# Moving the two-column carry copies of a fused attention and convolution kernel from GpSimd to ScalarE

## The chip, the cores and the metric

The kernel runs on one core of one Trainium2 chip. The metric is the device time of one execution in microseconds; the time before is the median of three runs.

## The reference

Eight batches (B = 8) of 8 heads with 512 tokens (x) and 32 state tokens (state), 64 wide, go through three blocks:

```python
# 1: attention between tokens and state, both ways
xread = softmax(scale * x @ state.T) @ state        # 512 rows per batch
sread = softmax(scale * state @ x.T) @ x            # 32 rows per batch
x = concatenate([xread, sread], axis=2)             # 544 rows per batch, 512 wide
# 2: gated convolution over the rows
h = maximum(x @ w_in, 0)                            # 1024 wide
conv_out = sum over k of conv_w[k] * hp[:, k:k + S] # 3 taps, hp is h with a zero row at each end
x = (h * sigmoid(conv_out)) @ w_out
# 3: a mix with the row before, then two products and a gate
k = maximum(xk @ w_k, 0); v = (k * k) @ w_v
out = sigmoid(xr @ w_r) * v
```

All arithmetic is held near float32: matrix products are made from a high and a low part of each operand, three products for one.

## The kernel before, in words

The second block is the part that the diff touches. Its rows are cut into nine tiles: tile t = 0 to 7 holds the 512 token rows of batch t, and the last tile (t = 8) holds the 32 state rows of all eight batches side by side. The 1024 columns of h are cut into eight groups f of 128, one group on the 128 partitions, so there are 72 slots (t, f), each of which passes these stages:

- `g1_main`: TensorE makes the product into the PSUM tile `hps`.
- `g1_a` (lines 486 to 512): GpSimd writes zeros to the first and last column of `hb` (L491), ScalarE writes relu of `hps` between them (L492), and GpSimd copies the last two columns of the block into `carry` (L493). In the last tile the two columns that precede each batch's 32 state rows are copied from `carry` into `hb` (L496, eight blocks of two columns), the pads behind them are zeroed (L497) and ScalarE writes the relu (L498). Then ScalarE makes the first tap of the convolution (L508, tile `cacc`) and VectorE adds the other two (L510).
- `g1_b`: ScalarE makes the tanh (L519), VectorE the gate (L520).
- `g1_c`: ScalarE makes the high part `gs` (L528); the low part (L530) is made by GpSimd for tiles 0 to 2 and by VectorE for the rest.
- `g1_sec`: TensorE multiplies `gs` by the output weights into the four accumulators `acc`; after the last f they are evicted (L549, L551) and stored.

`hb` has three buffers, so a slot's `hb` is free once VectorE's gate (L520) of three slots before has read it. The carry of all eight batches is read only in the last tile.

Between the slots the attention of the following batches is worked off in pieces (half slots): scores, maxima, exponentials (L361, L367, L377, L388 among them), and `pair_m`, which evicts a product (L283 on ScalarE, L284 on VectorE) and sends it to its place by four DMAs on SyncE's queue (L287). The next batch's `hps` reads it (tiles `me`, `m_odd`).

The order of instructions on each engine is not the order of the source. Each stage gets a priority, and a planner orders the queues along a timeline that it simulates itself:

```python
tc.cur_priority = BASE + 1000 * (i - d) + STAGE[k]                    # L1248
with _tile.TileContext(nc, schedule_with_timeline_sim=True) as tc:    # L1311
```

The third block (first 16 slots of the same form, then a stage of seven products per tile) doesn't contain the changed lines.

Of the kernel before, what the change touches and what calls it, by code (L numbers as in the profile page):

```python
# [11 lines left out]
AF = mybir.ActivationFunctionType  # L12
# [23 lines left out]
def tile_kernel(  # L36
# [26 lines left out]
    nc = tc.nc  # L63
    B, P, NST, H, D = x_n.shape
    KC, S = x_t.shape[1], x_t.shape[3]
# [54 lines left out]
    carry = const.tile([P, KF, B, 2], F32, name="carry")  # L120
# [339 lines left out]
    def width(t):  # L460
        return S if t < B else B * Z - 2
# [24 lines left out]
    def g1_a(t, f):  # L486
        n = width(t)
        s = st1[t, f]
        hb = s["hb"] = cp.tile([P, N + 2], F32, tag="hb", name="hb", bufs=3)
        if t < B:  # L490
            nc.gpsimd.memset(hb[:, 0:S + 2:S + 1], 0.0)  # L491
            nc.scalar.activation(hb[:, 1:1 + S], s["p"], AF.Relu)  # L492
            nc.gpsimd.tensor_copy(carry[:, f, t], hb[:, S - 1:S + 1])  # L493
        else:
            v = hb[:, :B * Z].rearrange("p (b n) -> p b n", b=B)
            nc.gpsimd.tensor_copy(v[:, :, 0:2], carry[:, f])  # L496
            nc.gpsimd.memset(v[:, :, NS + 2:], 0.0)  # L497
            nc.scalar.activation(  # L498
                v[:, :, 2:NS + 2], s["p"][:, :B * NS].rearrange("p (b n) -> p b n", b=B), AF.Relu
            )  # L500
        if t == 0 and f < CONV_ON_PE:
            a = s["a"] = ps_h.tile([P, 512], F32, tag="h", name="cps")
            for k in range(3):
                nc.tensor.matmul(a, diag[:, 3 * f + k], hb[:, k:k + S], start=k == 0, stop=k == 2)
            return
        a = s["a"] = cp.tile([P, N], F32, tag="acc", name="cacc")
        w = [vcol[:, k * KF + f:k * KF + f + 1] for k in range(3)]
        nc.scalar.activation(a[:, :n], hb[:, 0:n], AF.Copy, scale=w[0])  # L508
        for k in (1, 2):
            nc.vector.scalar_tensor_tensor(  # L510
                a[:, :n], hb[:, k:k + n], w[k], a[:, :n], op0=ALU.mult, op1=ALU.add
            )
# [682 lines left out]
    ]  # L1195
    end = len(slots)
    FN = {1: (g1_main, g1_a, g1_b, g1_c, g1_sec), 2: (g2_main, g2_a, g2_b, g2_c, g2_sec)}
    p2 = None
    for i in range(len(slots) + 2):
        if i < len(slots):  # L1200
            ph, t, f = slots[i]
# [113 lines left out]
```

## Time and profile before

| | |
|---|---|
| median of 3 runs | 848.87 us (847.53 to 849.36) |
| profiled execution | 847.36 us, of which 845.6 us lie between its first and last instruction |
| busy in the span: TensorE, VectorE, ScalarE, GpSimd | 815.8, 719.9, 601.3, 108.7 us |
| mean granted clock of TensorE | 0.993 |

The busy time of an engine is the union of its instructions; an engine that is busy all the time may still be slowed by waits inside, since ends of matmuls are modelled. The chain of waits is the chain of work that ended last, followed back from the last instruction of the program: at each step to what released it, or to the instruction before it on its engine. PE is TensorE's matmul, PEld its weight load, DVE is VectorE, ACT is ScalarE, POOL is GpSimd, SP is SyncE.

### The profile page before, as it was taken

Reading aid. Unit: us, or ns where it says so; the run is one execution under the profiler, and the core shown is the slowest. Engines: PE = TensorE matmul, PEld = TensorE weight load, DVE = VectorE, ACT = ScalarE, POOL = GpSimd, SP = SyncE. Lnnn points to the kernel's source line nnn. Section 1 sums busy time; section 2 is a strip of 40 time slices with the busy share of each in tenths; the row PEclk is TensorE's granted clock in tenths of the full one; section 3 lists DMA queues with packets and bytes.
Section 4 is the critical chain, followed back from the end, with each engine's and each line's share of the span. In section 5 each row is a group of like instructions: output and inputs, shape, how many; then the busy total and the mean of one; then the engine's idle time right before and its main releaser. Section 6 shows DMA issues by size and latency. Waiting matters only on the chain.

```text
span 845.6 us, 15284 instructions
## 1 busy us (share of the span) xinstructions
PE 815.8 (96%) x5670; PEld 718.1 (85%) x5670; DVE 719.9 (85%) x1143; ACT 601.3 (71%) x1035; POOL 108.7 (13%) x220
## 2 busy tenths in 40 slices
PE   5899999899989999999999989999999999999997
PEld 2466787678767877889989889999999999999997
DVE  6999987798999997989999889896978869696673
ACT  6787575586577756878877779767776876776652
POOL 2235453341111211211000000000000000000000
PEclk8999999999999999999999999999999999999999
DMA  9441436427673556405634765777778677775675
GB/s 335 143 152 51 153 92 192 126 68 207 216 214 125 177 173 205 194 3 200 228 121 162 251 235 172 253 240 246 252 227 268 214 237 262 221 257 180 220 240 205
DMA packets 82698, 163.10 MB, mean 193 GB/s; under 512 B 17600, under 2 KB 53440, under 8 KB 79808
## 3 DMA queue, kind: packets, MB, share of 16 engines
q1 hardware_dynamic: 82624, 162.12, 58.8%
q8 instruction: 45, 0.74, 0.4%
q14 instruction: 29, 0.24, 0.1%
HBM read 118.55 MB, written 30.97 MB: 177 GB/s over the span
## 4 chain that ended last, share of the span: by engine, by line
PE 74%; DVE 12%; DMA 6%; ACT 4%; issue 2%; SPq 2%; DVEq 0%; ACTq 0%; POOL 0%; POOLq 0%
PE acc L132 11%; PE acc L133 11%; PE acc L134 11%; PE vps L133 6%; PE vps L132 6%; PE vps L134 6%; PE rps L132 3%; PE rps L133 3%; PE rps L134 3%; PE hps L132 3%; PE hps L134 2%; PE hps L133 2%; DVE cacc L510 2%; DMA yt<-y 2%; DMA me<-m 1%
## 5 line engine op out<-in xcount | busy, mean ns | idle before, releaser
L510 DVE SCALAR_TENSOR_TENSOR cacc<-hb,vcol,cacc 128x512 f32<-128x512 f32 (+1 forms) x138 | 105.1, 775 | 6.2 <-ACT cacc L508 5.5
L133 PE MATMUL acc<-gs,out 128*128 128x512 f32 (+1 forms) x288 | 110.1, 384 | 0.2 <-POOL gs L530 0.2
L134 PE MATMUL acc<-gs,out 128*128 128x512 f32 (+1 forms) x288 | 109.0, 381 | 0.0
L132 PE MATMUL acc<-gs,out 128*128 128x512 f32 (+1 forms) x288 | 95.9, 385 | 0.8 <-ACT gs L528 0.8
L132 PEld LDWEIGHTS acc<-gs,out 128*128 128x128 f32 x288 | 53.0, 188 | 14.5 <-ACT gs L528 2.3
L132 PE MATMUL acc<-xo,k 128*128 128x256 f32 x224 | 63.2, 283 | 1.8 <-ACT xc L880 1.3
L133 PEld LDWEIGHTS acc<-gs,out 128*128 128x128 f32 x288 | 54.2, 188 | 10.9 <-POOL gs L530 0.6
L134 PEld LDWEIGHTS acc<-gs,out 128*128 128x128 f32 x288 | 54.2, 188 | 10.4 <-issue 0.5
L134 PE MATMUL acc<-xo,k 128*128 128x256 f32 x224 | 63.0, 282 | 0.0
L133 PE MATMUL acc<-xo,k 128*128 128x256 f32 x224 | 62.9, 281 | 0.0
L519 ACT ACTIVATE g<-cacc 128x512 f32<-128x512 f32 (+1 forms) x69 | 41.8, 606 | 24.8 <-DVE cacc L510 19.2
L528 ACT ACTIVATE gs<-g 128x512 fp32r<-128x512 f32 (+1 forms) x72 | 43.6, 607 | 21.9 <-DVE g L520 14.1
L520 DVE SCALAR_TENSOR_TENSOR g<-g,hb 128x512 f32<-128x512 f32 (+1 forms) x72 | 49.4, 686 | 1.8 <-ACT g L519 1.3
L492 ACT ACTIVATE hb<-hps 128x512 f32<-128x512 f32 x64 | 37.7, 593 | 17.8 <-PE hps L134 14.5
L508 ACT ACTIVATE cacc<-hb,vcol 128x512 f32<-128x512 f32 (+1 forms) x69 | 48.1, 703 | 1.3
L132 PE MATMUL acc<-xo,kT 128*128 128x256 f32 x168 | 47.8, 284 | 1.0 <-ACT acc L876 1.0
L133 PE MATMUL vps<-va,xa 128*128 128x256 f32 x168 | 47.6, 283 | 0.0
L132 PE MATMUL vps<-va,xa 128*128 128x256 f32 x168 | 47.5, 283 | 0.0
L134 PE MATMUL vps<-va,xa 128*128 128x256 f32 x168 | 47.5, 283 | 0.0
L133 PE MATMUL acc<-xo,kT 128*128 128x256 f32 x168 | 47.5, 283 | 0.0
L134 PE MATMUL acc<-xo,kT 128*128 128x256 f32 x168 | 47.5, 283 | 0.0
L493 POOL COPY carry<-hb 128x2 f32<-128x2 f32 x64 | 32.2, 504 | 97.2 <-ACT hb L492 97.0
(290 smaller groups left out, 2807.3 us busy)
## 6 DMA issues: line engine op xcount, KB each, us to landing
va<-vdT SPq DMA_DIRECT2D x38, 512.0 KB, 4.5
va<-vdB SPq DMA_DIRECT2D x28, 512.0 KB, 4.3
vb<-vdT SPq DMA_DIRECT2D x18, 512.0 KB, 4.6
xT<-x_t SPq DMA_DIRECT2D x32, 256.0 KB, 5.0
xn<-x_n SPq DMA_DIRECT2D x8, 1024.0 KB, 5.2
y<-yo SPq DMA_DIRECT2D x8, 1024.0 KB, 5.0
vb<-vdB SPq DMA_DIRECT2D x14, 512.0 KB, 4.2
va<-rdT SPq DMA_DIRECT2D x14, 512.0 KB, 4.5
```

The costliest lines, as they stand in the source:

```text
L132: nc.tensor.matmul(ps, lh, rh, start=start and k == 0, stop=False, **how)
L133: nc.tensor.matmul(ps, lh, rl, start=False, stop=False, **how)
L134: nc.tensor.matmul(ps, ll, rh, start=False, stop=stop and k == last, **how)
L492: nc.scalar.activation(hb[:, 1:1 + S], s["p"], AF.Relu)
L493: nc.gpsimd.tensor_copy(carry[:, f, t], hb[:, S - 1:S + 1])
L508: nc.scalar.activation(a[:, :n], hb[:, 0:n], AF.Copy, scale=w[0])
L510: nc.vector.scalar_tensor_tensor(a[:, :n], hb[:, k:k + n], w[k], a[:, :n], op0=ALU.mult, op1=ALU.add)
L519: nc.scalar.activation(g[:, :n], s["a"][:, :n], AF.Tanh, scale=0.5)
L520: nc.vector.scalar_tensor_tensor(g[:, :n], g[:, :n], 1.0, s["hb"][:, 1:1 + n], op0=ALU.add, op1=ALU.mult)
L528: act = nc.scalar.activation(gs[:, 0, :n], s["g"][:, :n], AF.Copy)
```

## The change

Both copies, the one into `carry` in tiles 0 to 7 (64 of them, 128x2) and the one out of it in the last tile (8 of them, 128x16), are made by an ACTIVATE of ScalarE with the function Copy in place of GpSimd's tensor_copy. The place in the source and the priority stay.

```diff
@@ g1_a @@
         if t < B:
             nc.gpsimd.memset(hb[:, 0:S + 2:S + 1], 0.0)
             nc.scalar.activation(hb[:, 1:1 + S], s["p"], AF.Relu)
-            nc.gpsimd.tensor_copy(carry[:, f, t], hb[:, S - 1:S + 1])
+            nc.scalar.activation(carry[:, f, t], hb[:, S - 1:S + 1], AF.Copy)
         else:
             v = hb[:, :B * Z].rearrange("p (b n) -> p b n", b=B)
-            nc.gpsimd.tensor_copy(v[:, :, 0:2], carry[:, f])
+            nc.scalar.activation(v[:, :, 0:2], carry[:, f], AF.Copy)
             nc.gpsimd.memset(v[:, :, NS + 2:], 0.0)
```

## Rows read from the trace of the kernel before

**Rows 1.** The page: busy time of the engines, and the chain by engine.

```profile
PE 815.8 (96%) x5670; PEld 718.1 (85%) x5670; DVE 719.9 (85%) x1143; ACT 601.3 (71%) x1035; POOL 108.7 (13%) x220
...
PE 74%; DVE 12%; DMA 6%; ACT 4%; issue 2%; SPq 2%; DVEq 0%; ACTq 0%; POOL 0%; POOLq 0%
```

**Rows 2.** Busy time by stage: stretch, length, then PE, PEld, DVE, ACT, POOL.

```profile
20.00:72.00 52.00, 47.27 (x244) 27.36 (x242) 51.82 (x67) 39.92 (x59) 17.41 (x18) 0.96 0.43 149
72.00:135.00 63.00, 62.81 (x439) 50.89 (x440) 56.55 (x89) 42.98 (x78) 29.20 (x49) 1.00 0.34 104
135.00:250.00 115.00, 110.08 (x721) 85.10 (x719) 100.41 (x177) 74.51 (x130) 29.43 (x56) 1.00 0.56 165
250.00:400.00 150.00, 147.91 (x882) 122.55 (x875) 139.91 (x240) 111.71 (x197) 27.16 (x71) 1.00 0.47 160
```

**Rows 3.** The same stretches for L493 alone: POOL busy and its copies.

```profile
20.00:72.00 52.00, 5.73 (x6) 0.96 0.43 149
...
135.00:250.00 115.00, 8.35 (x19) 1.00 0.56 165
```

**Rows 4.** The chain of waits, 135 to 250 us and later: start, length, what.

```profile
by line: DVE cacc L510 11.8%; issue 8.2%; SPq L287 7.5%; DMA m_odd<-m 7.3%; DVE g L520 7.2%; DMA me<-m 6.7%; DMA xT<-x_t 4.4%; DVE gs L530 3.4%; DVE s L385 3.3%; DVE m L284 2.6%; DVE q L357 2.3%; DVE s L360 2.1%; DVE s L348 2.1%; ACT m L283
...
157.61 4.39 DMA me<-m
...
184.44 0.49 ACT hb L492
...
197.94 6.06 DMA m_odd<-m
...
207.16 0.50 ACT hb L492
...
242.73 3.32 DMA me<-m
...
330.77 0.60 ACT hb L492
```

**Rows 5.** GpSimd's groups: busy, mean ns, then its idle time and what ended it.

```profile
L493 POOL COPY carry<-hb 128x2 f32<-128x2 f32 x64 | 32.2, 504 | 97.2 <-ACT hb L492 97.0
...
L496 POOL COPY hb<-carry 128x16 f32<-128x16 f32 x8 | 6.0, 745 | 20.2 <-DVE g L520 20.2
```

**Rows 6.** The tile carry: durations of its copies, and the only engine that waited.

```profile
L493 POOL COPY carry<-hb x64: 178/358/2459, 23.1 to 362.8; 128x2 f32<-128x2 f32 x64
...
  ACT g L519: 0.2, 1
```

**Rows 7.** ScalarE in order of time: start, duration, what.

```profile
3.03 0.22 ACT L178 ACTIVATE mid<-raw 128x24 f32<-128x24 f32 x1 [1.02 <-DMA raw<-conv]
3.16 0.21 ACT L180 ACTIVATE raw<-raw 128x24 uint32<-128x24 uint32 x1
...
265.65 0.19 ACT L367 ACTIVATION_READ_ACCUMULATOR e<-p_s,s 128x1 f32 x1
265.75 0.68 ACT L367 ACTIVATE e<-p_s,s 128x512 f32<-128x512 f32 x1
...
333.59 0.58 ACT L492 ACTIVATE hb<-hps 128x512 f32<-128x512 f32 x1
334.20 0.73 ACT L508 ACTIVATE cacc<-hb,vcol 128x512 f32<-128x512 f32 x1
```

**Rows 8.** A carry copy on GpSimd, and VectorE in order of time.

```profile
335.99 0.91 POOL L493 COPY carry<-hb 128x2 f32<-128x2 f32 x1 [0.98 <-ACT hb L492]
...
336.77 0.75 DVE L510 SCALAR_TENSOR_TENSOR cacc<-hb,vcol,cacc 128x512 f32<-128x512 f32 x1
337.43 0.69 DVE L520 SCALAR_TENSOR_TENSOR g<-g,hb 128x512 f32<-128x512 f32 x1
...
343.62 0.75 DVE L510 SCALAR_TENSOR_TENSOR cacc<-hb,vcol,cacc 128x512 f32<-128x512 f32 x1
344.29 0.69 DVE L520 SCALAR_TENSOR_TENSOR g<-g,hb 128x512 f32<-128x512 f32 x1
```

## The prediction

> **What bounds the kernel now.** I read the page first: TensorE is busy 96% of the span and takes 74% of the chain of waits, VectorE 12%, DMA 6%, ScalarE 4%, and GpSimd rounds to nothing [rows 1]. An average over stages with different limits is no price, so I then cut the stretch in which the changed lines run, 20 to 400 us, by stage [rows 2]. The reader is to see two kinds of stage there. From 72 to 135 us and from 250 to 400 us TensorE has work nearly without a break (62.8 of 63 us, 147.9 of 150 us): what another engine does there costs nothing until a weight load has to wait. From 20 to 72 us VectorE is the one without a break (51.8 of 52 us). From 135 to 250 us none is full (PE 110, VectorE 100, ScalarE 75 of 115 us), and the chain [rows 4] shows why: it hops from VectorE to SyncE's queue, to the landing of the small product that `pair_m` sends (4.39, 6.06 and 3.32 us), and back. Only in these two stages, 167 us together, can the change touch the path directly.
>
> Then I read who makes the copies and who needs them. The 64 copies into `carry` occupy GpSimd for 32.2 us, but before them it sat idle for 97.0 us, waiting for ScalarE's relu [rows 5]. Nobody waits for them but one tanh, once, for 0.2 us [rows 6]; the real reader is the last tile.
>
> **The change, part by part.**
>
> *GpSimd loses 64 + 8 copies*, 32.2 + 6.0 us of busy time [rows 5]. It is idle 87% of the span and the chain spends about 0% on it, so its own time is worth nothing. What stood behind a copy in its queue (the zeros of the next `hb`, the low parts of tiles 0 to 2) starts earlier by at most the copy, whose median is 0.36 us; the waits that this could shorten are not on the chain. I take 0.
>
> *VectorE might have been held up by them.* A copy lasts 178 ns at the least and 2459 ns at the most [rows 6], so something holds the copies, and they could hold VectorE in return. The rows decide this by the distance from the start of L510 to the start of the instruction behind it. In one case a copy runs from 335.99 to 336.90 us and so ends inside the L510 that starts at 336.77; the next instruction starts 0.66 us after that L510. In the other no copy is near, and the distance from 343.62 to 344.29 is 0.67 us [rows 8]. So the copy waits for VectorE, and VectorE does not wait for it: gain 0. The bound on the other side: had each copy held VectorE for its shortest duration, 0.178 us, in the two stages where VectorE or hops set the pace, 6 + 19 copies [rows 3] would give back 4.5 us.
>
> The Trainium skill's page "SBUF — State Buffer", section "Who interferes with whom", says that a VectorE instruction with two SBUF inputs and a GpSimd instruction that reads SBUF block one another entirely, the second to issue waiting for the first. The stretched copies fit that; the unchanged distance on VectorE does not show the other direction. By the rule taken both ways the sum would be lower by the 4.5 us above.
>
> *ScalarE gains 64 ACTIVATEs of two columns and 8 of sixteen.* The trace has none so small with this function, so I bound it. The nearest rows: an accumulator read of one column lasts 0.19 us, but the next instruction starts 0.10 us after it (265.65 to 265.75); an ACTIVATE of 24 columns lasts 0.22 us and the next starts after 0.13 us [rows 7]. So two columns push the queue by 0.10 us, sixteen by about 0.12 us (my estimate between these two). That is 64 x 0.10 + 8 x 0.12 = 7.4 us of queue time. The upper bound, with the whole 0.22 us counted for each, is 72 x 0.22 = 15.8 us. Both copies move no DMA and no wait on one.
>
> A wait is added: the copy reads what the relu just wrote. The next reader, L508, already has that wait: the relu of 333.59 ends at 334.17 and L508 starts at 334.20, so 0.03 us after it [rows 7]. A copy placed between them inherits this 0.03 us and pushes L508 by its 0.10 us. Queued behind it are L508, and the tanh (L519) and high part (L528) of the slots before, for which VectorE and then TensorE wait.
>
> How much of the 7.4 us shows? ScalarE is idle for 52 - 39.9 = 12 us, 20 us, 40 us and 38 us in the four stages [rows 2], and the 25 copies of the two stages off TensorE need 2.5 us of these. In the TensorE stages the product of one slot is consumed some slots later, and TensorE's continuous work hides a push of 0.1 us; were that cover gone, all 72 would show, 7.4 us. On the chain stand three relus between 135 and 250 us (184.44, 188.04 and 207.16, the first and last shown) and one at 330.77 [rows 4]. Behind each of these the copy is paid in full: 4 x 0.13 = 0.5 us. The other copies of these stages are hidden under VectorE; if they were not, 25 x 0.13 = 3.3 us.
>
> *In the last tile* ScalarE itself now stands where GpSimd stood, waiting for VectorE's gate to free `hb`: 20.2 us in eight waits, 2.5 us on average [rows 5]. The relu of the same slot needs that buffer as well, so a copy directly in front of it adds no wait; a copy queued earlier would add up to those 2.5 us for the tanh and high parts behind it. This lies in 250 to 400 us, under TensorE. I take 0 here.
>
> *The sum.* The profiled execution took 847.36 us (a span of 845.6 and 1.8 around it). 847.36 + 0 + 0 + 0.5 = 847.9 us. That execution lay 1.5 us below the median of the three runs, so on the median's scale it is 848.87 + 0.5 = 849.4 us. A difference of 0.2%, 1.7 us, is about what can be told from no change, as the three runs span 1.8 us.
>
> **What the sum leaves out** is the order. The queues are ordered by a planner along its own simulated time; 72 instructions that change engine shift that time, and the order of ScalarE's other instructions can change with it. No row of before prices this, so it enters through the rivals.
>
> **The rivals.**
>
> *Slower by order.* The place is the chain from 135 us to 330 us, where it passes four times through the product sent by `pair_m` (three landings stand in [rows 4], the fourth is like them). If in front of its eviction on ScalarE the planner now has one more instruction of 0.58 us, the length of a relu [rows 7], each pass is 0.6 us later: 4 x 0.6 + 0.5 = 2.9, so 851.8 us; with two, 5.3, so 854.2 us. It decides from three passes on (1.8 us). The wait of the last tile, placed too early, adds to the same side. For it: the chain has almost no slack there, and the new work goes to the engine that makes the eviction. Against it: ScalarE is idle for 40 of these 115 us.
>
> *Faster by order.* The same passes with one instruction fewer in front: 0.5 - 4 x 0.6 = -1.9, so 847.0 us, and 844.6 us with two. For it: nothing says that the order of before is the best one. Against it: the added work itself only delays.
>
> *Faster because VectorE is freed*, the skill's rule: 849.4 - 4.5 = 844.9 us. Against it stand the distances of [rows 8].
>
> **How the numbers follow.** The direct sum with little change of order: 0.40, at 849.4 us, its own range 847.5 to 851. Slower by order: 0.35, from 851 to 856. Faster by order: 0.18, from 844.5 to 847. VectorE freed: 0.07, near 845. So faster by over 0.2% 0.25, within it 0.40, slower 0.35. The range from 845 to 855 us leaves out about 1 in 10 on each side.
>
> **What would show it.** Right: GpSimd's busy time falls by about 38 us to 71; ScalarE's rises by 7 to 11; the new ACTIVATE lasts 0.19 to 0.22 us and pushes L508 by 0.1; VectorE's distances behind L510 stay at 0.66 us and its busy time in 20 to 400 us does not fall; the stages end within 1 us of where they ended. Wrong: a stage between 135 and 250 us that is longer or shorter by over 2 us, with the landings of `me` and `m_odd` on other places of the chain; weight loads of `acc` that wait for ScalarE's `gs` in the TensorE stages; or VectorE's L510 visibly shorter without the copies.

## The result and the profile after

The changed kernel takes 853.97 us (median of 9 runs, 850.62 to 855.09), the kernel before 848.28 us (9 runs, 846.0 to 849.36). The ratio of the means (853.04 to 848.13) is 1.0058 with a 95% interval of 1.0042 to 1.0074: slower, by 4.9 us. The range held it, on the side of the rival "slower by order" (0.35), and the likeliest case (849.4 us, no change) did not happen. The profiled execution took 854.12 us, a span of 852.3 us.

The page, after, beside [rows 1]: busy time of the engines, and the chain by engine.

```profile
PE 821.9 (96%) x5670; PEld 722.4 (85%) x5670; DVE 720.2 (84%) x1143; ACT 606.1 (71%) x1107; POOL 72.8 (9%) x148
...
PE 75%; DVE 13%; DMA 4%; ACT 3%; issue 2%; SPq 2%; POOL 0%; DVEq 0%; ACTq 0%; POOLq 0%
```

The work moved as the prediction says: GpSimd loses 35.9 us, ScalarE gains 72 instructions and 4.8 us, VectorE nothing. TensorE is busy 6.1 us more for the same 5670 matmuls, so it was slowed, and the other work does not show where. Busy time by stage, after, beside [rows 2] (stretch, length, then PE, PEld, DVE, ACT, POOL, granted clock, DMA share, GB/s):

```profile
20.00:72.00 52.00, 47.76 (x244) 28.48 (x242) 51.59 (x68) 40.45 (x66) 12.48 (x12) 1.00 0.44 150
72.00:135.00 63.00, 62.88 (x439) 50.89 (x440) 56.47 (x89) 44.21 (x90) 24.42 (x35) 1.00 0.34 104
135.00:250.00 115.00, 110.63 (x716) 84.23 (x714) 100.62 (x175) 74.81 (x146) 21.19 (x36) 0.99 0.55 162
250.00:400.00 150.00, 147.37 (x867) 121.70 (x868) 138.36 (x238) 112.69 (x228) 9.20 (x39) 1.00 0.46 158
400.00:474.00 74.00, 74.00 (x383) 66.68 (x382) 69.01 (x125) 58.31 (x121) 0.11 (x1) 1.00 0.52 177
474.00:505.00 31.00, 26.99 (x143) 23.55 (x142) 25.50 (x49) 18.67 (x40) 0.21 (x2) 0.89 0.81 280
```

The same last stretch before the change:

```profile
474.00:505.00 31.00, 28.29 (x188) 25.45 (x187) 25.93 (x48) 19.88 (x41) 0.10 (x1) 1.00 0.77 266
```

The four stages that hold the changed lines look much as they did, though 15 matmuls fewer are done from 250 to 400 us. The larger loss is at 474 to 505 us, in the third block, which holds no changed line: 45 matmuls fewer are done there, and the granted clock is 0.89 where it was 1.00. The start of the same matmul in both traces says how much: after is later by 2.0 us at 400 us, by 2.3 us at 470 us, by 6.6 us at 540 us, by 6.8 us at the end. Of the 2.3 us, 1.5 come at 158 to 170 us, where the granted clock is at half for 3.4 us after a wait for `me` that before has as well; the runs below show how much this early part varies from one execution to the next.

**Down to 5 us.** First after, then before:

```profile
485.00:490.00 5.00, 3.61 (x22) 2.78 (x21) 3.27 (x6) 3.42 (x9) 0.00 (x0) 1.00 0.74 274
490.00:495.00 5.00, 2.82 (x17) 2.09 (x17) 5.00 (x12) 2.21 (x5) 0.01 (x1) 0.97 0.95 315
495.00:500.00 5.00, 4.55 (x21) 4.55 (x22) 4.85 (x9) 2.00 (x4) 0.10 (x1) 0.50 1.01 350
500.00:505.00 5.00, 5.00 (x38) 5.00 (x38) 4.35 (x9) 4.58 (x11) 0.00 (x0) 0.84 0.74 270
```

```profile
485.00:490.00 5.00, 4.05 (x29) 3.52 (x30) 5.00 (x12) 3.79 (x8) 0.07 (x1) 1.00 0.78 238
490.00:495.00 5.00, 5.00 (x44) 5.00 (x44) 5.00 (x9) 2.32 (x4) 0.04 (x1) 1.00 0.93 319
495.00:500.00 5.00, 5.00 (x45) 5.00 (x44) 2.77 (x6) 2.66 (x6) 0.00 (x0) 1.00 0.64 238
500.00:505.00 5.00, 3.66 (x31) 3.45 (x30) 5.00 (x10) 5.00 (x11) 0.00 (x0) 1.00 0.32 127
```

TensorE is starved first (3.61 and 2.82 us busy of 5), and then runs five microseconds at a granted clock of 0.50, the 1.2 GHz level, so that a busy stretch does 21 matmuls instead of 45. A busy share of 4.55 hides this; the counts and the clock show it. Before has a gap of its own at 501 us (1.34 us), which after has not.

**Who starves it.** ScalarE in order of time (start, duration, line, what, count, and in brackets its idle time before and what ended it), before:

```profile
479.55 0.60 ACT L675 ACTIVATE r<-rps 128x512 f32<-128x512 f32 x1 [3.50 <-PE rps L134]
480.45 0.63 ACT L707 ACTIVATE xo<-flat 128x512 fp32r<-128x512 f32 x1 [0.31 <-PE acc L134]
481.80 3.31 ACT L630 ACTIVATE xb<-yt,om 128x352 f32<-128x352 f32 x8 [0.71 <-DMA yt<-y]
```

and after:

```profile
482.39 2.99 ACT L630 ACTIVATE xb<-yt,om 128x352 f32<-128x352 f32 x7 [4.01 <-DMA yt<-y]
485.29 0.58 ACT L675 ACTIVATE r<-rps 128x512 f32<-128x512 f32 x1
485.76 0.42 ACT L630 ACTIVATE xb<-yt,om 128x160 f32<-128x160 f32 x1
486.08 0.62 ACT L707 ACTIVATE xo<-flat 128x512 fp32r<-128x512 f32 x1
```

Before, the sigmoid (L675) and the high part `xo` (L707) went ahead of the eight mixes (L630), which wait for a load. After, the mixes stand first, and the two behind them wait 4.01 us for a DMA that they do not use. VectorE needs that `xo`. Before, then after:

```profile
481.12 0.69 DVE L708 TENSOR_TENSOR xo<-flat,xo 128x512 fp32r<-128x512 f32 x1 [1.77 <-ACT xo L707]
481.73 0.68 DVE L711 TENSOR_TENSOR tsum<-tsum 128x512 f32<-128x512 f32 x1
482.33 0.68 DVE L711 TENSOR_TENSOR flat<-xs,flat 128x512 f32<-128x512 f32 x1
```

```profile
486.73 0.69 DVE L708 TENSOR_TENSOR xo<-flat,xo 128x512 fp32r<-128x512 f32 x1 [4.71 <-ACT xo L707]
487.34 0.68 DVE L686 TENSOR_TENSOR r<-r,acc 128x512 f32<-128x512 f32 x1
487.94 0.69 DVE L708 TENSOR_TENSOR stage<-tsum,stage 128x512 fp32r<-128x512 f32 x1
488.54 0.68 DVE L711 TENSOR_TENSOR flat<-xs,flat 128x512 f32<-128x512 f32 x1
```

`xo` is 5.6 us later, and the sum `flat`, for which the next `xo` waits, is 6.2 us later (2.3 us of each were there at 470 us), with a gate and a `stage` now in front of it as well. TensorE's gaps of that time end on this chain (after):

```profile
488.17 0.36 PE L132 MATMUL acc<-xo,k 128*128 128x256 f32 x1 [1.35 <-DVE r L686]
...
495.45 0.58 PE L133 MATMUL acc<-xo,kT 128*128 128x256 f32 x1 [1.67 <-DVE xo L708]
```

The dependencies are those of before; the order in which the planner put the queues is not. On TensorE, VectorE and ScalarE most of the places at which it differs lie at 242 to 317 us and at 385 to 531 us, a few from 37 us on; on SyncE it differs from 406 us on.

**The copies themselves** (tile `carry` after, durations min/median/max in ns; beside [rows 6]):

```profile
L493 ACT ACTIVATE carry<-hb x64: 188/204/232, 23.2 to 365.0; 128x2 f32<-128x2 f32 x64
L496 ACT ACTIVATE hb<-carry x8: 199/204/237, 367.5 to 394.1; 128x16 f32<-128x16 f32 x8
```

One of them on ScalarE, between its relu and L508, beside [rows 7]:

```profile
335.58 0.57 ACT L492 ACTIVATE hb<-hps 128x512 f32<-128x512 f32 x1
336.18 0.20 ACT L493 ACTIVATE carry<-hb 128x2 f32<-128x2 f32 x1
336.30 0.71 ACT L508 ACTIVATE cacc<-hb,vcol 128x512 f32<-128x512 f32 x1
```

The copy starts 0.60 us after its relu, L508 0.72 us after it, where it was 0.61 us before: 0.11 us of push, for a duration of 0.20 us. And VectorE, beside [rows 8], keeps its distance of 0.67 us behind L510:

```profile
338.75 0.75 DVE L510 SCALAR_TENSOR_TENSOR cacc<-hb,vcol,cacc 128x512 f32<-128x512 f32 x1
339.42 0.68 DVE L520 SCALAR_TENSOR_TENSOR g<-g,hb 128x512 f32<-128x512 f32 x1
```

### The profile page after: what moved, and what is told of

It reads as the page before. It is cut to its first block, busy times and chain, and to the rows that moved or that the text cites. A ratio compares the mean times of both kernels' runs of the same rounds, so it can differ in the third digit from the quotient of the medians.

```text
span 852.3 us, 15275 instructions
## 1 busy us (share of the span) xinstructions
PE 821.9 (96%) x5670; PEld 722.4 (85%) x5670; DVE 720.2 (84%) x1143; ACT 606.1 (71%) x1107; POOL 72.8 (9%) x148
## 4 chain that ended last, share of the span: by engine, by line
PE 75%; DVE 13%; DMA 4%; ACT 3%; issue 2%; SPq 2%; POOL 0%; DVEq 0%; ACTq 0%; POOLq 0%
PE acc L133 11%; PE acc L134 11%; PE acc L132 11%; PE vps L133 6%; PE vps L132 6%; PE vps L134 6%; PE rps L133 3%; PE rps L134 3%; PE rps L132 3%; PE hps L132 2%; PE hps L134 2%; PE hps L133 2%; DVE cacc L510 2%; SPq L287 2%; PE kps L132 1%
## 5 line engine op out<-in xcount | busy, mean ns | idle before, releaser
L510 DVE SCALAR_TENSOR_TENSOR cacc<-hb,vcol,cacc 128x512 f32<-128x512 f32 (+1 forms) x138 | 104.3, 769 | 6.2 <-ACT cacc L508 5.6
L528 ACT ACTIVATE gs<-g 128x512 fp32r<-128x512 f32 (+1 forms) x72 | 43.5, 607 | 25.7 <-PE acc L134 14.7
L520 DVE SCALAR_TENSOR_TENSOR g<-g,hb 128x512 f32<-128x512 f32 (+1 forms) x72 | 49.5, 687 | 1.6 <-ACT g L519 1.0
L133 PE MATMUL acc<-xo,kT 128*128 128x256 f32 x168 | 48.8, 290 | 1.7 <-DVE xo L708 1.7
L132 PE MATMUL acc<-xo,kT 128*128 128x256 f32 x168 | 48.7, 290 | 1.0 <-ACT acc L876 1.0
L134 PE MATMUL acc<-xo,kT 128*128 128x256 f32 x168 | 48.6, 289 | 0.0
L508 ACT ACTIVATE cacc<-hb,vcol 128x512 f32<-128x512 f32 (+1 forms) x69 | 48.1, 698 | 0.2
L132 PEld LDWEIGHTS acc<-xo,k 128*128 128x128 f32 x224 | 42.4, 190 | 2.0 <-ACT stage L707 1.7
```

The lines of the kernel that those rows point to most:

```text
L132: nc.tensor.matmul(ps, lh, rh, start=start and k == 0, stop=False, **how)
L133: nc.tensor.matmul(ps, lh, rl, start=False, stop=False, **how)
L134: nc.tensor.matmul(ps, ll, rh, start=False, stop=stop and k == last, **how)
L510: nc.vector.scalar_tensor_tensor(a[:, :n], hb[:, k:k + n], w[k], a[:, :n], op0=ALU.mult, op1=ALU.add)
L520: nc.vector.scalar_tensor_tensor(g[:, :n], g[:, :n], 1.0, s["hb"][:, 1:1 + n], op0=ALU.add, op1=ALU.mult)
L528: act = nc.scalar.activation(gs[:, 0, :n], s["g"][:, :n], AF.Copy)
```

## The experiments

In runs 1 to 6 and 9 to 12 each engine's queue is held in a given order: a chain of edges orders the issue of its instructions, and no edge waits for anything. Such a list replaces the planner's choice, so that engine and order can be changed one at a time. (Imports and the packed list ORDER are left out here; the diffs of ORDER below are in words.)

```diff
+def pin(tc):
+    traced = {i.name: i for i in tc.nc.cur_bb.bb.instructions}
+    how = mybir.DependencyInfo(mybir.DependencyClass.NoSync, mybir.DependencyReason.DATA)
+    for queue in json.loads(zlib.decompress(base64.b85decode(ORDER))):
+        for a, b in zip(queue, queue[1:]):
+            tc.add_manual_dep(traced[f"I-{b}"], f"I-{a}", how, reason="pin")
...
         tile_kernel(tc, *args)
+        pin(tc)
```

All results in one table. A ratio is to the kernel before, run on the same chip with it. The other columns are of the one profiled execution: how much later than in before the same matmul starts at 470 and at 540 us, what this rose by, the sum of TensorE's idle stretches over 0.3 us that end between 480 and 525 us, and how long its granted clock was at half in a stretch that begins there.

| run | ratio [95%] | at 470 | at 540 | rise | idle | at half clock |
|---|---|---|---|---|---|---|
| before | 1 | 0 | 0 | 0 | 2.71 | 0 |
| after | 1.0058 [1.0042, 1.0074] | 2.32 | 6.56 | 4.24 | 3.98 | 6.8 |
| 1 copies ScalarE, order of before | 1.0004 [0.999, 1.0019] | -2.11 | -2.85 | -0.74 | 1.97 | 0 |
| 2 copies GpSimd, order of after | 1.007 [1.0049, 1.0091] | 2.72 | 6.17 | 3.45 | 4.40 | 3.4 |
| 3 order of after, then of before | 1.0014 [1.0, 1.0028] | 1.36 | -0.24 | -1.60 | 1.37 | 0 |
| 4 order of before, then of after | 1.0039 [1.0023, 1.0054] | 1.81 | 4.65 | 2.84 | 4.84 | 0 |
| 5 after, two moved | 1.0062 [1.0044, 1.008] | 2.26 | 4.53 | 2.27 | 3.48 | 3.4 |
| 6 before, two moved | 1.006 [1.0041, 1.0078] | -2.27 | 1.93 | 4.20 | 5.68 | 3.4 |
| 7 only the copies into `carry` | 1.0018 [1.0003, 1.0032] | 0.44 | 0.20 | -0.24 | 2.49 | 0 |
| 8 only the copies out of it | 1.0062 [1.0044, 1.0079] | -0.10 | 4.24 | 4.34 | 4.29 | 6.8 |
| 9 after, SyncE's tail of before | 1.021 [1.0187, 1.0234] | 8.11 | 18.61 | 10.50 | 10.14 | 6.8 |
| 10 after, the engines' tail of before | 1.0076 [1.0053, 1.0098] | 2.37 | 7.39 | 5.02 | 6.00 | 3.4 |
| 11 after, TensorE's tail of before | 1.0122 [1.0099, 1.0146] | -0.27 | 8.58 | 8.85 | 8.68 | 3.4 |
| 12 after, three moved | 1.0024 [1.001, 1.0037] | 0.24 | 1.91 | 1.67 | 2.64 | 3.4 |

Read the rise against the two columns beside it: the idle time beyond the 2.71 us of before, plus half of the time at half clock (an estimate: 21 matmuls were done at half clock where 45 were at the full one), gives it within 0.75 us in every row but run 11 (1.2 us): after 1.27 + 3.4 = 4.7 for 4.24, run 6 2.97 + 1.7 = 4.7 for 4.20, run 12 -0.07 + 1.7 = 1.6 for 1.67. So idle time and clock account for most of the tail's loss; what is left over was not traced.

Each row's profile is one execution, and not always a typical one: those of runs 1 and 6 are the fastest of their runs (844.51 and 849.27 us beside medians of 847.25 and 852.22), so the shifts and the ratio of a row need not agree. No run holds a kernel's own order unchanged; run 1 bounds what holding the queues costs together with the copies.

**Runs 1 and 2: the engine alone, the order alone.** Run 1 has the copies on ScalarE, each next to its relu, and every other instruction in the order of before. Run 2 has them on GpSimd, where the planner places them freely, and everything else in the order of after.

```diff
-ORDER = the planner's, with the copies on ScalarE
+ORDER = the planner's of before; each copy next to its relu on ScalarE
```

> Both copies on ScalarE as in the changed kernel, but every engine's queue is pinned to the order of the kernel before; a copy into carry stands right behind its relu, a copy out of it right in front of its relu. Theory A (the order that the planner chose is what costs): 0.5 us of direct cost, so 848.8 us, ratio to before 1.0006, at most 1.002. Theory B (ScalarE's 72 added instructions cost by themselves): about as slow as the changed kernel, 853 to 854 us, ratio 1.005 or more. ScalarE busy near 606 us in both.

```diff
-copies on ScalarE
+copies on GpSimd
 ORDER = the planner's of after, on all the other queues
```

> Both copies on GpSimd as in the kernel before, but the queues of all other engines are pinned to the order of the changed kernel, and GpSimd's other instructions too. Theory A (order): as slow as the changed kernel, 853 to 854 us, ratio 1.005 to 1.007. Theory B (ScalarE's added work): as fast as before, 848.3 us, ratio within 0.002 of 1.

Run 1 gives 847.25 us beside 846.83: 0.4 us. Run 2, without a single copy on ScalarE, loses 0.7%. This parts the two causes: moving the copies costs within -0.8 and +1.6 us, and the order alone costs as much as the whole change did. One part of the expectation missed: ScalarE is busy 610.7 us in run 1, where 606 were expected, and 600.4 us in run 2.

**Runs 3 and 4: which stretch of the order.** The copies are on ScalarE in both; the lists are cut at about 340 us, and the parts exchanged.

```diff
-ORDER = after
+ORDER = after up to 340 us, before from there
```

> Copies on ScalarE; the queues follow the changed kernel's order up to about 340 us (where both orders have done the same set of instructions on every engine) and the order of before from there. Theory A: only what the changed kernel had lost by then, 2.0 us by the starts of the same matmuls in the two traces, so 850.3 us, ratio 1.002. Theory B: 853 to 854 us, since nearly all copies (58 of 72) lie before the cut. A third way, that the part from 340 us on is slow whatever its order because of the state it starts from, would give 853 too.

```diff
-ORDER = after
+ORDER = before up to 340 us, after from there
```

> The reverse: the order of before up to about 340 us, the changed kernel's order from there, copies on ScalarE. Theory A: the 4 to 5 us that the changed kernel loses between 440 and 505 us, so 852.5 to 853 us, ratio 1.005, with the long gap of TensorE near 494 us in the trace. Theory B: 853 to 854 us. If the loss after 340 us came from the state at the cut and not from the order, it would be gone here: 848.8 us.

With the tail of before the loss is down to 0.14%; with the tail of after it is 0.39%, less than the 0.5% that was expected. The intervals overlap by 0.05% only, so the tail is the larger part. Whether the first part costs anything is not settled: 0.14% less the 0.04% of run 1 is 0.8 us, inside both intervals. Single profiles can't tell: the shift at 470 us scatters between -0.3 and 2.7 us among those with after's list up to 340 us (after, runs 2, 3, 5, 10, 11, 12), and as widely, between -2.3 and 1.8 us, among those with the list of before (before, runs 1, 4, 6).

**Runs 5 and 6: the head of ScalarE's queue.** Run 5 takes after's list and puts the sigmoid and `xo` ahead of the mixes, as before has them. Run 6 does the reverse to the list of before, with the copies still on GpSimd.

```diff
 ScalarE, order of after
+sigmoid r L675
+xo<-flat L707
 mixes xb L630 (7)
-sigmoid r L675
 mix xb L630
-xo<-flat L707
```

> The changed kernel with every queue pinned to its own order, but for two of ScalarE's instructions near 480 us: the sigmoid r (L675) and the first operand xo of the next tile (L707) stand in front of the eight mixes xb (L630), which wait for the load of yt, instead of behind seven and eight of them, as in the order of before. Theory C (head of line: ScalarE stands 4.0 us at the mixes while xo is due, and VectorE and TensorE wait for xo): most of what the part from 340 us on loses, about 3 of 4 us, comes back, so a ratio to before of 1.002 to 1.003. Rival D (the loss is spread over the other differences of the two orders): the ratio stays at 1.0055 to 1.006.

```diff
 ScalarE, order of before
-sigmoid r L675
-xo<-flat L707
 mixes xb L630 (7)
+sigmoid r L675
 mix xb L630
+xo<-flat L707
```

> The reverse: the kernel before, copies on GpSimd, all queues pinned to its own order, but the same two instructions of ScalarE put behind the mixes, as the changed kernel has them. Theory C: slower by about 3 us, ratio 1.003 to 1.004, with ScalarE idle for some 2 to 4 us in front of the first mix. Rival D: ratio 1.000 to 1.001.

Run 6 did more than expected: two instructions put behind a late load make the untouched kernel 0.6% slower, all that the whole change costs. Its ScalarE, and its VectorE and TensorE behind it:

```profile
479.96 2.99 ACT L630 ACTIVATE xb<-yt,om 128x352 f32<-128x352 f32 x7 [6.18 <-DMA yt<-y]
```

```profile
484.30 0.69 DVE L708 TENSOR_TENSOR xo<-flat,xo 128x512 fp32r<-128x512 f32 x1 [7.22 <-ACT xo L707]
```

```profile
486.93 0.47 PE L132 MATMUL acc<-xo,k 128*128 128x256 f32 x1 [4.71 <-ACT xo L707]
```

Run 5 missed: the two moves gave nothing back that can be told from noise (1.0062). So they suffice to make the loss and do not suffice to undo it. Its VectorE shows why, for `xo` is early again and `flat` is not:

```profile
483.38 0.69 DVE L708 TENSOR_TENSOR xo<-flat,xo 128x512 fp32r<-128x512 f32 x1 [1.26 <-ACT xo L707]
485.44 0.69 DVE L686 TENSOR_TENSOR r<-r,acc 128x512 f32<-128x512 f32 x1 [1.36 <-PE acc L134]
487.10 0.69 DVE L708 TENSOR_TENSOR stage<-tsum,stage 128x512 fp32r<-128x512 f32 x1 [0.97 <-ACT stage L707]
487.71 0.69 DVE L711 TENSOR_TENSOR flat<-xs,flat 128x512 f32<-128x512 f32 x1
```

The gate and the `stage`, which had stood unseen behind the late `xo`, now wait themselves (1.36 and 0.97 us), and `flat` comes 4.3 us after `xo` where it came 1.2 us after it in before.

**Runs 7 and 8: which copies upset the order.** The planner is free again; only one of the two lines is changed.

```diff
-            nc.gpsimd.tensor_copy(carry[:, f, t], hb[:, S - 1:S + 1])
+            nc.scalar.activation(carry[:, f, t], hb[:, S - 1:S + 1], AF.Copy)
```

> Only the 64 copies into carry go to ScalarE; the 8 copies out of it stay on GpSimd; the planner is free. It leaves sigmoid and xo in front of the mixes and SyncE's queue as before; orders differ from before only in the second block's part. Theory C: 0.4 us of direct cost and what the changed order before 340 us loses, ratio 1.001 to 1.0015. Rival B (added ScalarE work is the cost, 64 of 72 instructions): ratio 1.005.

```diff
-            nc.gpsimd.tensor_copy(v[:, :, 0:2], carry[:, f])
+            nc.scalar.activation(v[:, :, 0:2], carry[:, f], AF.Copy)
```

> Only the 8 copies out of carry go to ScalarE, the planner is free. It puts sigmoid and xo behind the mixes as in the changed kernel. Theory C: the loss from 340 us on, ratio 1.0035 to 1.004. Rival B (8 of 72 instructions, 1 us of ScalarE's time): ratio 1.000 to 1.001.

The 64 copies, 13.0 of the 14.7 us of new work, keep the order of before in the tail (VectorE's from 386 us on, ScalarE's from 384) and cost 0.18%. The eight copies, some 0.2 us each, leave every queue ahead of 365 us as in before, bring nearly the order of after behind that, and with it the whole loss: 0.62%. So the order behind 365 us is enough for it, with the order of before ahead. The cost does not go with the work added, but with where the planner's timeline tips over. Run 8 was expected at 1.0035 to 1.004, from what run 4 had shown.

**Runs 9 to 11: one queue's tail at a time.** After's lists, but from 340 us on (SyncE: 406 us) some queues in the order of before.

```diff
 ORDER = after
+SyncE from 406 us on: before
```

> The changed kernel with every queue held in its own order, but SyncE's queue from about 406 us on in the order of before (which loads of yt and which stores of stage come first). Theory Q (the loss of the third block sits in the queues of ScalarE, VectorE and TensorE, where instructions that wait stand in front of ready ones): 1.005 to 1.006 of before, little changed. Theory S (the loads of yt are issued late behind other DMAs, and all else follows from that): about 1.0015, as with the whole tail of before.

```diff
 ORDER = after
+TensorE, VectorE, ScalarE from 340 us on: before
```

> The complement: from about 340 us on TensorE's, VectorE's and ScalarE's queues in the order of before, SyncE's in the order of after. Theory Q: about 1.0015 of before, as with the whole tail of before. Theory S: 1.005 to 1.006, little changed.

```diff
 ORDER = after
+TensorE from 340 us on: before
```

> The changed kernel held in its own order, but TensorE's queue from about 340 us on in the order of before. Theory Q says that TensorE waits for the results of the other two and that its own order is a follower: 1.005 to 1.008 of before, no gain. If TensorE's order is itself the cause: 1.002 or less.

Both theories missed: none of these three parts of the better order, set into the worse one, helps; run 10 is at 1.0076, and the other two are much slower (1.021 and 1.0122). The trace of run 10 tells how. Up to 499 us it stays at the shift that it had at 470 (2.37 us): with the three engines in the order of before, the stall of 480 to 495 us is gone, as theory Q has it. Then ScalarE waits 6.06 us where before waits 2.53 us at the same place:

```profile
503.23 1.12 ACT L630 ACTIVATE flat<-yt,om 128x384 f32<-128x384 f32 x2 [6.06 <-DMA yt<-y]
```

SyncE, in the order of after, issues this load at 495.45 us, behind a store that waits for a `stage`; in before it goes out at 489.88. After's own engines want it later. In these runs the queues of one plan fit each other, and no single one of them is "the cause". In run 9 ScalarE stands 7.15 us at the mixes for `yt`, whose load is issued at 482.90 us, and at 503 to 511 us another 7.63 us for a load of `vdT`; what slows run 11 was not followed.

**Run 12: the three waits together.** Run 5, and VectorE's `flat` directly behind the `xo` that it follows.

```diff
 VectorE, order of after (ScalarE as in run 5)
 xo<-flat,xo L708
+flat<-xs,flat L711
 r<-r,acc L686
 stage<-tsum,stage L708
-flat<-xs,flat L711
```

> As the run with two instructions of ScalarE moved in front of the mixes (1.0062, no gain), and VectorE's sum flat, for which the next xo waits, directly behind the xo that it follows in before (it stood behind one gate and one stage). If these three head-of-line waits are what the tail costs: 1.002 to 1.004. If others take their place again, as they did with two: 1.005 to 1.006.

It recovers the larger part: 1.0024. Of some 1100 instructions on either queue three stand elsewhere than in after, and 0.34 of the 0.58% is gone. Its windows:

```profile
490.00:495.00 5.00, 3.32 (x21) 3.11 (x21) 5.00 (x10) 0.64 (x2) 0.10 (x1) 0.83 0.95 370
495.00:500.00 5.00, 5.00 (x37) 5.00 (x37) 4.17 (x7) 4.32 (x10) 0.00 (x0) 0.83 1.01 326
```

Its idle time is that of before (2.64 and 2.71 us); what is left is one stretch of 3.4 us at half clock, after a gap of 1.68 us that VectorE's `xo` of L708 ends. By the table that is 1.7 us, and the ratio is 2.0 us. No version tried beats the kernel before; the nearest are runs 1 and 3.

## Why the prediction was right in its range and wrong in its likeliest case

- **GpSimd, 0.** Right: 35.9 us less busy time, and nothing gained by it in run 1.
- **VectorE not held, 0.** Right. The distance behind L510 stays at 0.67 us, and run 1 does not show a gain of 4.5 us. The one pair of rows that decided it stands for the rest: in the trace of before, the 24 L510 with a carry copy as the only GpSimd instruction beside them last 747 ns in the median, and those with no GpSimd instruction beside them 743. The rule cited from the Trainium skill, "SBUF — State Buffer", section "Who interferes with whom", that a two-input VectorE instruction and a GpSimd one that reads SBUF block each other, would give that gain; of the copies only GpSimd's side of it shows, stretched to 2459 ns [rows 6]. The other side shows beside longer instructions of GpSimd, which the change leaves where they are: all 15 of L510 and L520 that last over 0.9 us in before overlap one of these. VectorE's gate, for instance, takes 1.77 us beside a low part (L530) and 0.68 us elsewhere:

```profile
84.74 1.85 POOL L530 TENSOR_TENSOR gs<-g,gs 128x512 fp32r<-128x512 f32 x1 [0.58 <-ACT gs L528]
```

```profile
85.36 1.77 DVE L520 SCALAR_TENSOR_TENSOR g<-g,hb 128x512 f32<-128x512 f32 x1
```

- **ScalarE, 7.4 us of queue time, 0.5 us exposed.** Right: 0.11 us of push for a copy, taken as 0.10; 0.4 us in run 1, whose interval is -0.8 to 1.6. The busy time rose by 4.8 us and not by 7 to 11; with the order of before it rises by 9.4 us (run 1), so this sign too depended on the order. Why it is less in the order of after was not taken apart.
- **The last tile, 0.** Right for its waits: of all readers of `carry` only one weight load waited, 0.8 us once. But its eight copies are what tips the order (run 8).
- **What the sum leaves out.** This is the step that failed. The order was left at 0 in the likeliest case, and it was 4.9 us, all of the result but for what the interval of run 1 leaves to the copies. The sign "the stages end within 1 us of where they ended" failed with it: after is 2.0 us late at 400 us.
- **Slower by order.** The rival was right in its sign and size (851 to 856 us), and wrong in its place, so that the size fits is luck. It was put on the four passes through `pair_m` at 135 to 330 us, near the changed lines and where the chain had least slack. TensorE's busy time shows next to nothing there (110.63 for 110.08 us, 147.37 for 147.91 us), what the stretch lost in the profiled execution is within the scatter of runs 3 and 4, and most of the loss is at 480 to 505 us, where none of the changed instructions runs. The mechanism was that of the rival, an instruction in front that should stand behind, but one that waits for a load rather than one that takes 0.58 us; so its price was about 4 us at once (run 6) and not 0.6 us a pass.
- **A price it had no term for**: the clock. By the table's estimate, 4.7 us for a rise of 4.24 in after's tail, 3.4 us are TensorE's stretch at half clock and 1.3 us the added gaps.

What stays open: whether the first part of the order costs 0 or about 1 us (run 7, which has the copies into `carry` and only that part, is slower by 0.03 to 0.32%); why run 5, which had 2 us less loss in its profiled tail than after, was no faster over all its executions; and what in the planner's timeline the eight copies shift. Only its outcome was seen.

## What to carry to other kernels

Where a planner orders the queues from a timeline of its own, price an edit twice: once for its work and once as a new order, and look for the second far behind the edited lines, wherever a queue holds instructions that wait for a late transfer in front of others that are ready. To part the two, hold the queues in a recorded order and change one thing; and do not expect one queue of a good plan to help in another plan, since here the queues fit each other. Where a gap of TensorE is followed by a stretch at half clock in a kernel's own rows, price that stretch too.

## What the hardware showed that was not expected

In after, TensorE had gaps of 3.98 us in all between 486 and 496 us, none of them longer than 1.67 us. From 494.7 us on its granted clock stood at 0.50 (1.2 GHz) for 6.8 us, which by the table's estimate cost 3.4 us, more than the 1.3 us of added gaps. It is not a fixed price: run 12 had 3.4 us of it with 2.64 us of gaps, before had none with 2.71 us, and run 4 none with 4.84 us. In the other stretch, after had 3.4 us of it behind a gap of 2.04 us at 160 us, and before none behind one of 2.10 us at the same place.
